# One core: attention by packed keys, then a gated two-layer product, with another table of the order of the same 2739 pieces

## The chip, the cores and the metric

The kernel runs on one core of a Trainium2 chip. The metric is device time in microseconds (us) of one execution. The engines named here are TensorE (PE; its weight loads are shown apart as PEld), VectorE (DVE), ScalarE (ACT) and SyncE (SP), whose only work is to issue the DMAs.

## What is computed

Eight batches of eight heads attend through 32 packed queries `p`: first `p` looks at `k` and `v`, and then `q` looks at what that gave. The rows of all heads side by side are `x` (4608 x 512), which goes through a gated pair of matrix products.

```python
def sm_attn(qq, kk, vv):
    s = scale * np.matmul(qq, kk.transpose(0, 1, 3, 2))
    s = s - np.max(s, axis=-1, keepdims=True)
    a = np.exp(s)
    a = a / (np.sum(a, axis=-1, keepdims=True) + 1e-09)
    return np.matmul(a, vv)
p_packed = sm_attn(p, k, v)          # 8 x 8 x 32 x 64
out = sm_attn(q, p_packed, p_packed) # 8 x 8 x 576 x 64
...
h = x @ w_in                         # 4608 x 2048
sp = np.where(h > 20.0, h, np.log1p(np.exp(np.minimum(h, 20.0))))
g = h * np.tanh(sp)
return (g @ w_out).astype(np.float32)
```

Inputs and output are float32; `w_in` and `w_out` come to the kernel as the 64-bit patterns of doubles and are turned into float32 by it.

## The kernel before

**Pieces and their order.** The function `program()` (L1073) builds a list of 2739 pieces with a `Lineup` (L184). `add` gives each piece its engine, what it reads, writes and takes of buffers, and its number. 904 pieces are for PE, 728 for DVE, 701 for ACT and 406 for SP. `Lineup.sequence` (L216) walks the table `SEQUENCE` (L40 to L176) and issues the pieces in its order. Every engine then carries out its own pieces in that order and nothing else decides: a piece whose input is late holds up all that stands behind it on its engine, and a DMA on SP holds up all DMAs behind it. The tile framework puts the waits in, and hands out the buffer of a kind that became free first.

```python
        for n in numbers:
            if n < 0:
                yield from [fill] * -n
                continue
```

**Fills.** A negative number in the table is that many fills (L1556, L1557): products of the identity with itself into a bank of PSUM that nobody reads. They occupy PE where it would wait. Each shows as two matmul records of 128 columns.

**The attention of a batch.** For batch 0 `first(b)` and for the others `later(b)` add these pieces: `s` (scores, L359), `mx` and `top` on DVE (L402 to L409, the maxima), `tl` on ACT (L312, one tiny exponential that makes ACT fetch its table for exp), `e` on ACT (L421, four exponentials from PSUM), `w` on PE (L452, turning), `a1T` (L478, L481), `pv` (L487, L502), `pp` (L520), `ppTp`/`ppT` (L529, L535), `m` (L540, the matches with `q`), then `rm`, `rl`, `rs2`, `ri`, `wg` on DVE and `e2` on ACT (the second softmax; for batch 1 L617 to L647 with L634 on ACT, for the others L561 to L584 with L571), `tw` (L604) and `aT` (L661, L664).

**The weights.** `fetch` (L698) brings a piece of `w_in` or `w_out`. `up`, `sg`, `rn`, `bd` and `w`/`wi` turn it into float32: `up` L704 and `rn` L714 on ACT, `sg` L708, `bd` L717 and `w` L723 on DVE. `wo` (L742) and L745 split `w_out` into a high and a low part, which are kept in DRAM (`w_f32`, `quarters`, L750 and L755). `again` (L811) brings a piece of `w_in` once more. `pw` (L825) multiplies a piece of `w_in` into the packed values; `wph` (L844, ACT) and `wp` (L849, DVE) split the result into high and low.

**The first two batches** go by blocks. An `up` piece (L884) makes the gate's input; `act` (L890, and L892 for the rest) is the Mish function on ACT; L896 and L900 split it; `down` (L932 to L934) multiplies by `w_out`. `up` writes to one of two PSUM banks in turn, `ps_h` and `ps_x`; `ps_x` also holds the scores of a batch (`s`) until its `e` pieces have read them.

**Batches 2 to 7** go by steps with mixed quarters of `w_out`. `L774` to `L791` make the mixtures from `mix_w` (fetched at L768) with ACT's part at L782 and DVE's at L786, and store them. L798 brings a mixture for each step (`mix`, 512 KB). A step is `sup` (L974), `sx` (L980, ACT) and `sh` (L982), sums (L995 to L999), a split (L1003 on ACT, L1007 on DVE), `sdown` (L938 to L940) and endings (L1027 on ACT, L1033 on DVE), then a send (L1039, L1044).

**Table loads of ACT.** Exp and Mish lie in different tables. A table is loaded ahead of the first activation of the other kind; `tl` pieces stand there so that this load is not made by the `e` or `e2` piece itself.

Of the kernel before, what the change touches and what calls it, by code (L numbers as in the profile page):

```python
# [40 lines left out]
    1, 0, 2, 6, 5, 107, 64, 7, 8, 3, 9, -3, 12, 10, 11, 13, 4, 14, -1, 19, 15, 65, 16, 20, -4, 21, 17, 18, 25, 22, 23,  # L41
    26, 24, 66, 109, 27, 28, 29, 113, 110, -2, 30, 120, 31, 108, -2, 32, 126, 111, 33, 69, 35, 112, 34, 162, 38, 36, 37,
    39, 75, -1, 44, 41, 40, 42, 70, 47, 45, 43, 46, 176, -7, 71, 48, 51, 49, 182, 115, 114, 72, 116, 50, 195, 121, 122,
    -6, 55, 73, 123, 189, 127, 74, 76, 128, 78, 52, 79, 67, 124, 77, 53, 80, 125, 129, -11, 83, 54, 163, 68, 117, 58, 56,
    164, 85, 61, 81, 86, 130, 84, 82, 165, 131, -3, 87, 213, 118, 177, 59, 166, 178, 88, 167, 179, -3, 133, 57, 62, 132,
    183, 63, 60, 136, 184, 134, 119, 137, 185, 135, 168, 233, 191, 138, 190, 186, 170, 192, 193, 253, 196, 194, 140, 139,
    340, 197, 180, 273, 181, 89, 141, 187, 144, 198, 430, 199, 90, 146, 200, 142, 423, 145, 215, 202, 214, 143, 147, 169,
    150, 216, 217, 203, 152, 218, 205, 204, 221, 172, 151, 148, 188, 206, 173, 153, 287, 235, 154, 91, 149, 234, 155,
    219, 237, 156, 236, 92, 254, 174, 238, 157, 158, 299, 220, 239, 255, 207, 159, 93, 201, 209, 208, 257, 256, 240, 223,
    241, 210, 94, 224, 96, 225, 258, 243, 274, 95, 261, 244, 160, 259, 320, 245, 277, 97, 161, 175, 275, 260, 227, 276,  # L50
    98, 211, 229, 228, 288, 99, 278, 263, 291, 100, 281, 226, 279, 417, 230, 246, 369, 280, 300, 264, 231, 212, 265, 289,
    301, 101, 302, 247, 303, 102, 249, 322, 304, 323, 283, 292, 307, 321, 284, 262, 232, 248, 305, 324, 285, 250, 325,
    251, 267, 306, 341, 266, 103, 326, 308, 269, 268, 252, 436, 344, 309, 328, 270, 342, 600, 271, 290, 310, 343, 104,
    370, 418, 419, 345, 105, 286, 327, 420, 311, 272, 346, 329, 330, 348, 424, 425, 347, 171, 331, 426, 484, 106, 350,
    431, 504, 427, 373, 293, 428, 371, 352, 432, 294, 421, 433, 295, 434, 351, 353, 498, 313, 437, 374, 222, 296, 332,
    422, 297, 438, 354, 314, 440, 439, 372, 315, 355, 298, 511, 312, 486, 485, 333, 441, 487, 435, 356, 316, 517, 318,
    488, 443, 429, 357, 604, 499, 500, 365, 319, 501, 366, 505, 506, 529, 334, 489, 507, 508, 492, 336, 513, 335, 539,
    502, 514, 599, 381, 503, 337, 358, 338, 512, 339, 367, 518, 549, 519, 360, 515, 490, 442, 516, 520, 382, 521, 446,
    368, 642, 509, 444, 383, 447, 359, 361, 531, 375, 363, 491, 530, 377, 364, 532, 533, 392, 376, 534, 559, 384, 541,
    540, 537, 385, 445, 601, 542, 543, 393, 522, 378, 379, 394, 544, 550, 380, 387, 547, 386, 535, 551, 402, 643, 552,  # L60
    403, 545, 569, 396, 388, 523, 390, 536, 404, 644, 553, 560, 554, 398, 561, 524, 645, 562, 391, 646, 413, 647, 563,
    397, 414, 648, 555, 564, 395, 399, 650, 649, 406, 400, 557, 570, 605, 408, 401, 407, 546, 746, 454, 527, 556, 525,
    405, 567, 409, 526, 448, 411, 573, 565, 450, 579, 528, 449, 571, 455, 451, 651, 464, 606, 652, 415, 572, 607, 602,
    456, 608, 655, 465, 610, 609, 611, 412, 466, 656, 474, 613, 653, 657, 614, 458, 658, 612, 654, 416, 615, 603, 459,
    460, 452, 453, 457, 317, 574, 747, 461, 510, 581, 580, 462, 468, 582, 463, 470, 469, 478, 471, 659, 480, 475, 750,
    467, 660, 589, 389, 748, 476, 661, 479, 751, 477, 663, 662, 481, 749, 494, 664, 618, 482, 666, 495, 577, 621, 619,
    665, 583, 712, 620, 566, 802, 575, 622, 472, 349, 473, 616, 617, 496, 591, 623, 576, 497, 592, 624, 722, 625, 667,
    626, 584, 713, 671, 627, 723, 590, 672, 674, 706, 668, 628, 673, 708, 884, 707, 483, 714, 629, 709, 818, 724, 410,
    715, 669, 710, 716, 670, 711, 718, 717, 630, 732, 719, 726, 675, 742, 727, 728, 720, 679, 721, 631, 733, 593, 680,
    682, 725, 594, 803, 632, 597, 734, 681, 729, 633, 883, 758, 548, 242, 736, 676, 738, 585, 677, 743, 730, 806, 678,  # L70
# [101 lines left out]
    2686, 2622, 2680, 2694, 2688, 2623, 2689, 2624, 2695, 2690, 2681, 2696, 2625, 2703, 2682, 2626, 2691, 2665, 2704,  # L172
    2666, 2692, 2698, 2705, 2699, 2706, 2700, 2708, 2713, 2709, 2710, 2714, 2701, 2717, 2702, 2711, 2718, 2712, 2715,
    2721, 2722, 2719, 2723, 2725, 2726, 2729, 2727, 2731, 2730, 2716, 2733, 2720, 2735, 2724, 2732, 2728, 2737, 2734,
    2736, 2738,
)  # L176

F64_SCALE = 2.0 ** -112
# [1453 lines left out]
```

## Time and profile before

| what | value |
|---|---|
| time of the runs | 693.58, 691.81, 692.48 us; median 692.48 |
| span of the profiled execution | 691.1 us |
| time of its own for the profiled execution | none shown; its span is 1.4 us under the median of the runs |
| PE busy | 674.8 us, 98% |
| DVE busy | 501.7 us, 73% |
| ACT busy | 409.3 us, 59% |
| moved by DMA | 200.26 MB, mean 290 GB/s |

The span is from the first to the last instruction that the profiler saw. Busy times of different engines overlap each other. Matmuls on PE are pipelined: the next one starts before the one before it has ended, so the start-to-start time is what one costs.

### The profile page before, as it was taken

The page shows a single profiled execution, that of the slowest core. Times are in us where ns is not written, and L with a number is a line of the kernel's source. Part 1 is how long each engine was busy: PE and PEld are TensorE (multiplying, and loading weights), DVE is VectorE, ACT ScalarE, POOL GpSimd, SP SyncE. Part 2 cuts the span into 40 slices and gives each one's busy share as a digit, 9 for nine tenths or more (in the row PEclk, how much of TensorE's full clock was granted, in tenths as well). Part 3 has the DMA queues.
Part 4 walks back from the last instruction along what each step waited for, and adds up shares of the span by engine and source line. Part 5 has one row for each costly group of instructions (what it writes and reads, how often), then busy time and mean ns, then how long its engine had stood idle before and what let it go on. Part 6 is the DMA issues. An engine that isn't in the chain of part 4 may idle for free.

```text
span 691.1 us, 15614 instructions
## 1 busy us (share of the span) xinstructions
PE 674.8 (98%) x6144; PEld 611.1 (88%) x6144; DVE 501.7 (73%) x999; ACT 409.3 (59%) x900; POOL 0.7 (0%) x6
## 2 busy tenths in 40 slices
PE   8889999999999999999999999999999999999997
PEld 5668787778789999999999999899999999899996
DVE  2999996788655786578886686868766777665674
ACT  4899998554543655556666465666555545444552
POOL 0000000000000000000000000000000000000000
PEclk9999999999999999999999999999999999999999
DMA  8998999999999977794989827787496918481866
GB/s 300 402 407 294 345 378 355 328 347 344 370 397 418 386 238 305 251 359 155 346 280 340 307 103 265 296 287 292 141 403 221 360 44 294 151 289 60 312 204 216
DMA packets 70569, 200.26 MB, mean 290 GB/s; under 512 B 7776, under 2 KB 22112, under 8 KB 70496
## 3 DMA queue, kind: packets, MB, share of 16 engines
q1 hardware_dynamic: 70496, 199.26, 79.2%
q8 instruction: 49, 0.80, 0.4%
q14 instruction: 24, 0.20, 0.1%
HBM read 164.63 MB, written 34.60 MB: 288 GB/s over the span
## 4 chain that ended last, share of the span: by engine, by line
PE 78%; DMA 12%; DVE 4%; ACT 3%; issue 1%; SPq 0%; DVEq 0%; ACTq 0%
PE ps_h L974 20%; PE acc L938 13%; PE acc L939 12%; PE acc L940 12%; PE ps_h L884 5%; DMA mix<-mixed 4%; PE ps_w L825 4%; PE acc L932 3%; PE acc L933 3%; PE acc L934 3%; DMA mixed<-mix_o 2%; DMA w_out_f<-wo 1%; PE ps_s L359 1%; DMA xT<-in_q_rest_dram 1%; DMA wi<-w_in_f 1%; DMA xT<-in_q_main_dram 1%
## 5 line engine op out<-in xcount | busy, mean ns | idle before, releaser
L938 PE MATMUL acc<-mix,mixed_split 128*128 128x256 f32 x784 | 225.1, 287 | 1.3 <-DMA mix<-mixed 1.0
L939 PE MATMUL acc<-mix,mixed_split 128*128 128x256 f32 x784 | 221.7, 283 | 0.0
L940 PE MATMUL acc<-mix,mixed_split 128*128 128x256 f32 x784 | 221.6, 283 | 0.0
L974 PE MATMUL ps_h<-aT_hi,wp 128*128 128x256 f32 (+1 forms) x768 | 174.0, 297 | 0.0
L1007 DVE TENSOR_TENSOR mixed_split<-x,mixed_split 128x896 fp32r<-128x896 f32 x112 | 121.6, 1088 | 58.9 <-ACT mixed_split L1003 57.9
L938 PEld LDWEIGHTS acc<-mix,mixed_split 128*128 128x128 f32 x784 | 149.8, 191 | 15.0 <-issue 10.0
L1003 ACT CAST mixed_split<-x 128x896 fp32r<-128x896 f32 x112 | 105.3, 941 | 85.2 <-DVE x L999 47.6
L940 PEld LDWEIGHTS acc<-mix,mixed_split 128*128 128x128 f32 x784 | 150.2, 192 | 0.0
L939 PEld LDWEIGHTS acc<-mix,mixed_split 128*128 128x128 f32 x784 | 150.0, 191 | 0.0
L980 ACT ACTIVATE x<-ps_h 128x256 f32<-128x256 f32 x192 | 72.5, 384 | 101.9 <-PE ps_h L974 97.8
L974 PEld LDWEIGHTS ps_h<-aT_hi,wp 128*128 128x128 f32 x768 | 131.2, 190 | 0.6 <-issue 0.5
L974 PE MATMUL ps_h<-aT_lo,wp 128*128 128x320 f32 (+1 forms) x384 | 113.6, 296 | 0.0
L995 DVE TENSOR_TENSOR x<-x 128x128 f32<-128x128 f32 x112 | 32.0, 286 | 59.2 <-ACT x L980 58.0
L974 PEld LDWEIGHTS ps_h<-aT_lo,wp 128*128 128x128 f32 x384 | 73.0, 190 | 0.1
L884 PE MATMUL ps_h<-aT_hi,wp 128*128 128x288 f32 x256 | 58.8, 299 | 4.6 <-ACT g L890 1.6
L884 PEld LDWEIGHTS ps_h<-aT_hi,wp 128*128 128x128 f32 x256 | 43.5, 188 | 11.0 <-ACT wp L844 2.1
L932 PE MATMUL acc<-wo,split 128*128 128x512 f32 x128 | 51.4, 402 | 0.0
L996 DVE TENSOR_TENSOR x<-x 128x256 f32<-128x256 f32 x112 | 47.6, 425 | 5.0
L933 PE MATMUL acc<-wo,split 128*128 128x512 f32 x128 | 50.2, 392 | 0.0
L934 PE MATMUL acc<-wo,split 128*128 128x512 f32 x128 | 50.1, 392 | 0.0
L849 DVE TENSOR_TENSOR wp<-ps_w,wp 128x512 fp32r<-128x512 f32 x64 | 42.2, 681 | 8.9 <-ACT wp L844 8.7
L1033 DVE TENSOR_TENSOR o<-acc,o 128x256 f32<-128x256 f32 x98 | 38.7, 416 | 10.5 <-PE acc L940 8.3
(106 smaller groups left out, 822.9 us busy)
## 6 DMA issues: line engine op xcount, KB each, us to landing
mix<-mixed SPq DMA_DIRECT2D x141, 512.0 KB, 6.8
wi<-w_in_f SPq DMA_DIRECT2D x56, 512.0 KB, 7.5
mix<-shared SPq DMA_DIRECT2D x17, 512.0 KB, 8.9
xT<-in_k_main_dram SPq DMA_DIRECT2D x16, 512.0 KB, 5.8
v<-in_v_main_dram SPq DMA_DIRECT2D x16, 512.0 KB, 8.1
w_st<-in_w_in_dram SPq DMA_DIRECT2D x16, 512.0 KB, 7.4
xT<-in_q_main_dram SPq DMA_DIRECT2D x16, 512.0 KB, 7.9
w_st<-in_w_out_dram SPq DMA_DIRECT2D x16, 512.0 KB, 7.9
```

The costliest lines, as they stand in the source:

```text
L884: nc.tensor.matmul(out=ps, lhsT=w[:, fs], rhs=a[:, g, cs], start=(n == 0), stop=(n == 5))
L932: nc.tensor.matmul(out=acc, lhsT=hi[:, cs], rhs=wh, start=start, stop=False)
L933: nc.tensor.matmul(out=acc, lhsT=hi[:, cs], rhs=wl, start=False, stop=False)
L934: nc.tensor.matmul(out=acc, lhsT=lo[:, cs], rhs=wh, start=False, stop=stop)
L938: nc.tensor.matmul(out=acc, lhsT=hi, rhs=w[:, 0], start=start, stop=False)
L939: nc.tensor.matmul(out=acc, lhsT=hi, rhs=w[:, 1], start=False, stop=False)
L940: nc.tensor.matmul(out=acc, lhsT=lo, rhs=w[:, 0], start=False, stop=stop)
L974: nc.tensor.matmul(out=ps, lhsT=w[:, fs], rhs=x[:, g, a:e], start=(n == 0), stop=(n == 5))
L980: nc.scalar.activation(out=self.x[:, at:at + 2].rearrange("p c t -> p (c t)"), in_=self.ps[i][:, :m], func=AF.Mish)
L996: nc.vector.tensor_tensor(out=x[:, 1:3], in0=x[:, 3:8:4], in1=x[:, 6:7].to_broadcast([P, 2, P]), op=ALU.subtract)
L1003: nc.scalar.copy(out=self.split[:, 0], in_=self.x[:, :7])
L1007: nc.vector.tensor_tensor(out=x[:, 1], in0=self.x[:, :7], in1=x[:, 0].bitcast(F32), op=ALU.subtract)
```

## The change

Only the table `SEQUENCE` is another one. It holds the same 2739 pieces, each once; the code, the buffers and the dependencies are as they were. The fills are 27 in 9 places in place of 43 in 11. Of the pieces, 501 of 904 on PE keep their order among each other, 459 of 701 on ACT, 412 of 728 on DVE and 237 of 406 on SP. On PE no piece moves by more than 11 places.

```diff
@@ -38,141 +38,147 @@
 SEQUENCE = (
-    1, 0, 2, 6, 5, 107, 64, 7, 8, 3, 9, -3, 12, 10, 11, 13, 4, 14, -1, 19, 15, 65, 16, 20, -4, 21, 17, 18, 25, 22, 23,
-    26, 24, 66, 109, 27, 28, 29, 113, 110, -2, 30, 120, 31, 108, -2, 32, 126, 111, 33, 69, 35, 112, 34, 162, 38, 36, 37,
-    39, 75, -1, 44, 41, 40, 42, 70, 47, 45, 43, 46, 176, -7, 71, 48, 51, 49, 182, 115, 114, 72, 116, 50, 195, 121, 122,
-    -6, 55, 73, 123, 189, 127, 74, 76, 128, 78, 52, 79, 67, 124, 77, 53, 80, 125, 129, -11, 83, 54, 163, 68, 117, 58, 56,
-    164, 85, 61, 81, 86, 130, 84, 82, 165, 131, -3, 87, 213, 118, 177, 59, 166, 178, 88, 167, 179, -3, 133, 57, 62, 132,
-    183, 63, 60, 136, 184, 134, 119, 137, 185, 135, 168, 233, 191, 138, 190, 186, 170, 192, 193, 253, 196, 194, 140, 139,
-    340, 197, 180, 273, 181, 89, 141, 187, 144, 198, 430, 199, 90, 146, 200, 142, 423, 145, 215, 202, 214, 143, 147, 169,
...
-    460, 452, 453, 457, 317, 574, 747, 461, 510, 581, 580, 462, 468, 582, 463, 470, 469, 478, 471, 659, 480, 475, 750,
-    467, 660, 589, 389, 748, 476, 661, 479, 751, 477, 663, 662, 481, 749, 494, 664, 618, 482, 666, 495, 577, 621, 619,
-    665, 583, 712, 620, 566, 802, 575, 622, 472, 349, 473, 616, 617, 496, 591, 623, 576, 497, 592, 624, 722, 625, 667,
...
-    1251, 1230, 1249, 1252, 1255, 1250, 1167, 1257, 1256, 1253, 1163, 1168, 1272, 1258, 1259, 1169, 1265, 1203, 1166,
...
-    1504, 1597, 1500, 1443, 1508, 1505, 1521, 1531, 1605, 1444, 1506, 1512, 1513, 1509, 1608, 1514, 1510, 1445, 1517,
-    1446, 1609, 1515, 1447, 1518, 1448, 1610, 1516, 1527, 1519, 1611, 1522, 1523, 1520, 1606, 1449, 1524, 1528, 1450,
...
+    1, 0, 2, -1, 7, 5, 8, 9, 10, 11, -1, 12, 13, 14, 6, 15, 16, 19, -3, 21, 23, 17, 20, 18, 25, 22, 107, 24, 109,
+    26, 27, 28, 3, 29, -1, 30, 108, 31, 111, 110, -1, 32, 112, 33, 4, 35, 113, 115, 64, 34, 36, 37, 38, 44, 39, 41,
+    40, 42, 45, 114, 75, 117, 47, 48, 65, 43, 66, 46, 96, 116, 118, 120, 51, 126, 122, 121, -6, 71, 72, 73, 123,
+    127, 128, 74, 129, 76, 80, 78, 162, 124, 69, 77, 79, 49, 164, 165, 176, 50, -11, 55, 56, 52, 83, 81, 70, 53,
+    125, 54, -2, 58, 163, 61, 85, 84, 178, 179, 86, 82, 182, 189, 59, 130, 177, 87, 88, 417, 166, 195, 131, 183,
+    167, 184, 185, 57, -1, 133, 62, 60, 191, 180, 213, 136, 137, 134, 63, 135, 138, 192, 140, 190, 139, 67, 68, 181,
+    196, 193, 273, 89, 197, 198, 186, 144, 141, 90, 187, 146, 199, 194, 200, 215, 142, 143, 202, 168, 169, 145, 214,
...
+    453, 467, 460, 494, 459, 468, 461, 746, 574, 579, 602, 575, 470, 581, 576, 462, 582, 463, 580, 469, 747, 471,
+    472, 478, 480, 750, 658, 659, 479, 476, 657, 481, 751, 748, 663, 749, 583, 473, 654, 603, 495, 496, 523, 664,
+    616, 712, 618, 620, 660, 477, 706, 621, 619, 713, 565, 714, 584, 617, 538, 622, 661, 585, 666, 578, 665, 587,
...
+    1167, 1272, 1168, 1169, 1170, 410, 1249, 1254, 1172, 1173, 1273, 1283, 1284, 1175, 1259, 1261, 1203, 1174, 1176,
+    1265, 1260, 1266, 1267, 1268, 1250, 1262, 1294, 1274, 1276, 1204, 1275, 1269, 1277, 1179, 1182, 1270, 1181,
...
+    1449, 1617, 1618, 1450, 1632, 1548, 1633, 1549, 1550, 1551, 1553, 1636, 1637, 1547, 1624, 2122, 1552, 1638,
...
```

Some stretches of the two tables, read engine by engine (number:piece; the batch, block or step stands first in the brackets):

```
SP, first DMAs
before  1:k(0,0) 0:pT(0) 2:k(0,1) 6:v(0,1) 5:v(0,0) 107:fetch(0) 64:pT(1) 3:q(0,0) 4:q(0,1) 65:k(1,0) 66:k(1,1) 113:fetch(1) 120:fetch(2) 126:fetch(3)
after   1:k(0,0) 0:pT(0) 2:k(0,1) 5:v(0,0) 6:v(0,1) 107:fetch(0) 3:q(0,0) 4:q(0,1) 113:fetch(1) 64:pT(1) 65:k(1,0) 66:k(1,1) 120:fetch(2) 126:fetch(3)
ACT, from the second softmax of batch 0 to the first gates
before  47:e2(0) 51:e2(0) 114:up(1) 116:rn(1) 121:up(2) 123:rn(2) 127:up(3) 78,79,77,80:e(1) 129:rn(3) 163:up(4) 56:aT 85,84:a1T(1) 165:rn(4) 177:up(5) 59:aT 88:pp(1) 179:rn(5) 62:aT 183:up(6) 136,134:wph(0) 185:rn(6) 168:wo(0) 190:up(7) 192:rn(7) 196:up(8) 139:act(0) 141:act(0) 198:rn(8) 90:ppT(1) 142:gh(0)
after   114:up(1) 75:tl(1,0) 47:e2(0) 96:tl(1,1) 116:rn(1) 51:e2(0) 121:up(2) 123:rn(2) 127:up(3) 129:rn(3) 80,78,77,79:e(1) 165:rn(4) 56:aT 163:up(4) 85,84:a1T(1) 179:rn(5) 59:aT 177:up(5) 88:pp(1) 183:up(6) 185:rn(6) 62:aT 136,134:wph(0) 192:rn(7) 190:up(7) 139:act(0) 196:up(8) 198:rn(8) 141:act(0) 90:ppT(1) 142:gh(0) 168:wo(0)
DVE, second softmax of batch 0
before  39:rm 40:rl 42:rm 45:rm 43:rl 46:rl 48:rs2 49:ri 115:sg(1) 72:mx(1)
after   115:sg(1) 39:rm 40:rl 42:rm 45:rm 117:bd(1) 48:rs2 43:rl 46:rl 118:w(1) 122:sg(2) 72:mx(1)
PE, around w(2)
before  747:pw(6) 468:up(18,0) 470:up(18,1) 478:up(19,0) 480:up(19,1) 475:down(15,1) 467:down(14,3) 476:down(15,2) 477:down(15,3) 494:down(16,0) 618:w(2)
after   747:pw(6) 478:up(19,0) 480:up(19,1) 476:down(15,2) 495:down(16,1) 496:down(16,2) 712:down(17,0) 618:w(2)
PE, scores of batch 4 to the next piece that takes ps_x
before  1167:s(4) 1253:sdown(15,2) 1272:sdown(16,0) 1265:sup(19,0) 1283:sdown(17,0) 1273:sdown(16,1) 1254:sdown(15,3) 1274:sdown(16,2) 1294:sdown(18,0) 1267:sup(19,1)
after   1167:s(4) 1272:sdown(16,0) 1254:sdown(15,3) 1273:sdown(16,1) 1283:sdown(17,0) 1284:sdown(17,1) 1265:sup(19,0) 1267:sup(19,1)
ACT, exponentials of batch 4
before  1266:sx(19) 1171:tl(4,0) 1173,1174,1176,1175:e(4) 1268:sx(19)
after   1238:sh(17) 1249:sh(18) 1173,1175,1174,1176:e(4) 1266:sx(19) 1268:sx(19)
PE, from the piece that frees the buffer of mixture 1450 to the piece that uses it
before  1520:sdown(34,3) [14 pieces, 9.0 us of PE] 1632:sdown(39,0)
after   1520:sdown(34,3) [20 pieces, 14.5 us of PE] 1632:sdown(39,0)
SP, around the piece of w_in fetched again for pw(10)
before  790:send quarters(7) 829:again(10) 787:send quarters(4) quarters(5) 830:again(11) 781:send 927:mix(0,1) 928:mix(0,2)
after   927:mix(0,1) 928:mix(0,2) quarters(7) rk(0) quarters(7) 929:mix(0,3) 930,931:mix(1) 781:send 932:mix(1,2) 829:again(10) 830:again(11) 933:mix(2,0)
```

The `tl` pieces stand elsewhere too: in the table after, `e` of batches 3, 4, 6 and 7 and `e2` of batches 3 to 7 have no `tl` directly ahead of them that would load their table, and three `tl` pieces stand between Mish pieces. By the order of the pieces on ACT, its table has to be changed 33 times where it was 27 (with one load at the start that both have, 28 loads are in the profile of before).

## Rows read from the trace of the kernel before

**Rows 1.** The page: busy time, share and instructions of each engine.

```profile
PE 674.8 (98%) x6144; PEld 611.1 (88%) x6144; DVE 501.7 (73%) x999; ACT 409.3 (59%) x900; POOL 0.7 (0%) x6
```

**Rows 2.** Busy time by stretch: start:end, length, engines, granted PE clock, DMA share, GB/s.

```profile
34.60:51.80 17.20, 14.77 (x125) 11.80 (x126) 16.41 (x33) 16.50 (x37) 0.00 (x0) 1.00 1.03 406
...
34.00:36.00 2.00, 0.67 (x3) 0.44 (x4) 1.68 (x4) 2.00 (x4) 0.00 (x0) 1.00 1.01 351
```

**Rows 3.** Waits of PE up to 42 us: waited for, us in total, times, longest.

```profile
PE ps_h L884 <- ACT g L890: 1.6, 1, 1.6
...
PE ps_h L884 <- ACT wp L844: 1.2, 1, 1.2
PE ps_h L884 <- DVE wp L849: 0.8, 1, 0.8
```

**Rows 4.** Waits of PE after 42 us, all of them.

```profile
PE acc L938 <- DMA mix<-mixed: 1.0, 3, 0.5
PE ps_a L452 <- DVE wp L849: 0.8, 1, 0.8
PE ps_h L884 <- ACT g_rest L892: 0.5, 2, 0.3
PE ps_h L884 <- ACT a L421: 0.5, 1, 0.5
PE acc L938 <- DVE o L1033: 0.2, 1, 0.2
```

**Rows 5.** ACT in order of time, 19 to 39 us: start, length, instruction, idle before.

```profile
19.58 0.63 ACT L634 ACTIVATE a<-a 128x512 f32<-128x512 f32 x1 [1.58 <-DVE a L623]
...
35.02 0.62 ACT L742 CAST wo<-wo 128x512 fp32r<-128x512 f32 x1
35.51 0.70 ACT L704 ACTIVATE wi<-w_st 128x512 f32<-128x512 f32 x1
...
36.90 0.65 ACT L704 ACTIVATE wi<-w_st 128x512 f32<-128x512 f32 x1
37.57 1.28 ACT L890 ACT_TABLE_LOAD   x1
38.86 0.66 ACT L890 ACTIVATE g<-ps_h 128x288 f32<-128x288 f32 x2
```

**Rows 6.** PE in order of time, at 39, 41, 126, 193, 278 and 286 us.

```profile
39.33 0.40 PE L884 MATMUL ps_h<-aT_hi,wp 128*128 128x288 f32 x1 [1.65 <-ACT g L890]
...
41.12 1.09 PE L825 MATMUL ps_w<-wi,ppT 64*32 64x512 f32 x16
...
126.43 1.09 PE L452 MATMUL ps_a<-ident,a 128*128 128x128 f32 x8 [0.82 <-DVE wp L849]
...
193.88 1.95 PE L825 MATMUL ps_w<-wi,ppT 64*32 64x512 f32 x32
...
278.77 1.31 PE L359 MATMUL ps_s<-xT,pT 64*32 64x256 f32 x32
...
286.59 0.28 PE L974 MATMUL ps_h<-aT_hi,wp 128*128 128x256 f32 x1
```

**Rows 7.** DVE in order of time, at 122 us.

```profile
122.97 0.69 DVE L774 TENSOR_TENSOR mix_t<-mix_w 128x512 f32<-128x512 f32 x1 [3.35 <-DMA mix_w<-w_out_f]
```

**Rows 8.** The chain that ended last: start, length, what (a mixture at 361 us).

```profile
360.94 9.09 DMA mix<-mixed
```

**Rows 9.** DVE and ACT in order of time around the exponentials of batch 4.

```profile
282.65 0.17 DVE L409 TENSOR_SCALAR top<-top 128x2 f32<-128x2 f32 x1
...
285.67 0.53 ACT L421 ACTIVATE a<-ps_s,top 128x320 f32<-128x320 f32 x1
```

**Rows 10.** SP in order of time, at 183 us.

```profile
183.01 1.59 SPq L811 DMA_DIRECT2D wi<-w_in_f x2
```

**Rows 11.** The page: DMA issues: out<-in, engine, op, count, KB each, median us to landing.

```profile
wi<-w_in_f SPq DMA_DIRECT2D x56, 512.0 KB, 7.5
```

**Rows 12.** DVE in order of time, from 681 us.

```profile
684.39 2.66 DVE L1033 TENSOR_TENSOR o<-acc,o 128x256 f32<-128x256 f32 x7 [4.36 <-PE acc L940]
```

250 rows, old and new, of the table SEQUENCE are left out of this document.

## The prediction

> **What bounds the kernel now.** I read the busy times first: PE is busy for 674.8 us of the 691.1 us span [rows 1], so a new order can only win what PE loses to waits, and can lose whatever it adds to them. Second, the stretches: from 34.6 to 51.8 us PE is busy for 14.77 of 17.20 us while ACT and DVE are nearly full (16.50 and 16.41) [rows 2]. There the chain through ACT sets the pace. Third, the waits of PE, parted at 42 us. Before it, three waits between 33 and 40 us are on ACT's and DVE's work on the first packed weights and gates: 1.6, 1.2 and 0.8 us [rows 3]. After it there are eight waits of together 3.0 us [rows 4]. That view counts from the modelled end of the matmul before; by starts, each costs some 0.16 us more (the wait of 0.82 us at 126.43 us is one of 0.98), so the eight cost about 4.3 us. This is nearly all that the order after 42 us has to give: the rest of PE's time is products that both tables hold, and switches between kinds of products, as many of them in either.
>
> **What the change does, part by part.**
>
> *The start.* After the second softmax of batch 0 the order before puts, between the split of the first packed weights and the first gate, two `rn`, one `wo`, two `up` and the table load on ACT. The new table takes `wo(0)` out and puts `up(8)` behind the first gate. By starts, `wo` costs 35.51 - 35.02 = 0.49 us (the next piece follows at once) and `up` 37.57 - 36.90 = 0.67 us [rows 5]; the pieces of `rn` only change places. Further ahead, `up(1)` and `rn(1)` move into holes in which ACT waits for the softmax's first step on DVE (1.58 us before 19.58) [rows 5]. They would give 1.2 us, but `sg(1)`, `bd(1)` and `w(1)` now stand among the softmax pieces on DVE and take most of that back; walking both engines piece by piece with durations of their rows, I keep 0.35 us. So the first gate comes at 38.86 - 0.49 - 0.67 - 0.35 = 37.35 us. The second gate of that pair is now behind `up(8)` and `rn(8)`, at 37.35 + 0.33 + 1.31 = 38.99, and frees `ps_x` some 0.47 us later, at 39.46. Before, PE went through that block without a second stop, from 39.33 to `pw(1)` at 41.12, so its second half, 0.89 us, began at 40.23 [rows 6]. The difference is **-0.77 us**. Nothing hides this, as PE waits here; how long it lasts is decided by whether `fetch(1)` lands in time, since `sg(1)` reads it at the head of DVE's softmax. `fetch(1)` moves ahead of three transfers on SP, so it should. The bounds: both holes used and no delay of the softmax, a gain of 0.77 + 0.85 = 1.6 us; or `sg(1)` held for some 0.8 us, a gain of nought.
>
> *Sixteen fills less.* They stand in waits. Where the wait is longer than they are they cost nothing, and their going gains nothing: 0, with bounds of 0 and -0.5 us.
>
> *Mixtures that came late.* Three waits of 1.0 us together are for a mixture of 512 KB [rows 4]. At 361 us a transfer takes 9.09 us from issue to landing, [rows 8], with 9.0 us of PE pieces between the release of its buffer and its use: it lands just too late. The new table has 14.5 us of pieces there, and similarly 17.3 for 10.8 us at the second such wait (595 us). Two of three go; the third, the last mixture of all, has 9.0 us of PE work in both tables. **-0.96 us** (of the 1.0 + 3 x 0.16 us, the part of the first two, 0.42 and 0.54).
>
> *Waits behind mix_w.* At 122.97 us DVE had stood for 3.35 us at a difference, waiting for `mix_w` [rows 7], with the low half of `wp` behind it, for which PE's turning `w(2)` stood 0.82 us [rows 6]. An earlier such wait held the maxima of batch 2, hence the exponentials and `ps_x`, 0.5 us [rows 4]. In the new table those differences stand later against their fetches by 0.5 to 6 us of work, with one exception (three us, after the last of those waits). I take both as gone, -0.98 and -0.56 (0.5 with its 0.16, shorter by rounding), and of the two waits on `g_rest` half, -0.2: **-1.74 us**. But `w(2)` stands only 4.3 us of PE work behind `pw(6)`, where it was 6.6; the bound on the other side is that it keeps its whole wait.
>
> *Table loads.* ACT changes its table 33 instead of 27 times, at 1.28 us each [rows 5]: 7.7 us more on an engine with 40% to spare [rows 1]. Three pairs stand in stretches where ACT has idle time, and are costed at nothing; the cover is the idle time of ACT between gates. The other side is what has lost its `tl`. The next piece on `ps_x` after the scores of batch 4 comes 3.96 us of PE work after them, and was at 286.59 with scores until 278.77 + 1.31 = 280.08, so 6.5 us [rows 6]. The chain that must fit is maxima and top (in the trace until 282.82, with DVE's endings between them; about 1.5 us alone), four exponentials (at most 0.53 us each, overlapping a little, 1.9 us) [rows 9], and now the load, if it begins only after `top`: 3.4 + 1.28 = 4.6 us. It overruns by 0.7 us in batch 4, and is even in batches 6 and 7 (4.68 us of cover). Where the load goes ahead of the wait, it costs nothing. I take **+0.7 us**; bounds 0 and +3.
>
> The Trainium skill, page "ScalarE: Activation LUTs", section "What ACT_TABLE_LOAD costs", gives 1283 ns for the load plus about 1380 ns of drain, 2.66 us a switch. The trace's load agrees, but the activation after it starts 1.29 us after the load's start (38.86 - 37.57) [rows 5], so no such drain follows it here; by the page's total the overrun of batch 4 would be 2.1 us rather than 0.7 and the sum 1.4 us worse.
>
> *w_in fetched again for pw(10).* The two transfers left SP from 183.01 for 1.59 us [rows 10]; a transfer of `wi` takes a median of 7.5 us from issue to landing [rows 11], so the second landed before 192, and `pw(10)` began at 193.88 [rows 6], some 2 us to spare. The new table puts five to eight mixtures ahead. At 406 GB/s [rows 2] a mixture is 1.3 us, 6 to 10 us in all, against a queue whose mixtures may leave as soon as their buffers are free, so much of it moves into time that SP spent waiting. Bounds 0 and +6, taken **+0.2** (the row nearest: it had landed before `pw` was reached).
>
> *The end.* The last endings run 684.39 to 687.05 [rows 12] and the same pieces stand there, but one that was between them is now earlier, so the chain hangs on an earlier piece: **+0.2 us**, bounds 0 and +0.4.
>
> Sum: -0.77 - 0.96 - 1.74 + 0.7 + 0.2 + 0.2 = -2.37 us on the span, 691.1 to 688.7 us. The profiled execution stands 1.4 us under the median of the runs, 692.48, so the median comes to 692.48 - 2.37 = **690.1 us**, -0.34%. About 0.3%, 2.1 us, is what a measurement of this kernel can tell from no change.
>
> **The rivals.**
>
> *Given back.* The eight waits are what is left of many places where margins are near nought, and a table of other margins makes new ones of the same size: 4.3 us before, 4.3 us after, less the start and the added terms. For it: PE's distance from scores to the next `ps_x` piece falls in batches 4 to 7, and from `pw(6)` to `w(2)`. Against it: most mixtures get longer distances. It gives -0.77 + 0.2 = -0.6, 691.9 us.
>
> *Slower by table loads.* One mechanism: an `e` or `e2` piece without `tl` starts the load after DVE's result, with DVE's endings (0.41 us each) in between as in batch 4. Then scores to exponentials takes 4.6 + 0.8 = 5.4 us against a cover of 4 to 4.7, and the second softmax carries 1.28 us likewise. Four `e` and five `e2` pieces at 0.7 to 1.3 us are up to 9 x 1.0 = 9 us. It decides once more than 5 of those nine reach PE: the forecast without its +0.7 is -3.1, and 6 x 1.0 turns it into +2.9, 695.4 us. For it: ACT's place in the scores' chain is fixed. Against it: PE has `sdown` pieces to do in batches 3 to 7 and its own waits there were for transfers alone [rows 4].
>
> *The clock.* With 16 fills fewer, PE is idle longer before 33 us. The trace shows a granted clock of 1.00 (2.4 GHz) even from 34 to 36 us, with 0.67 of 2.00 us busy [rows 2], so I see no sign that it falls. If it fell to 1.2 GHz from 24 to 34 us, the scores, turnings and values there (some 4 us at full clock) would take 4 us more, half of it hidden by ACT: +2, 692.1 us. The Trainium skill, page "TensorE: Matmul & The Clock Gate", section "Part 1: The HAM clock gate", has an idle PE fall back to half its clock; by it the fewer fills could do this, and rows 2 show no such fall at the idlest stretch.
>
> **How the numbers follow.** Forecast 0.48 (its own range 688.3 to 691.3), given back 0.33, slower by table loads or by the late `pw(10)` 0.13, the clock 0.06. Half of the forecast's neighbourhood lies on either side of the bound of 0.3% (690.4), but the early gain and the mixtures may be larger than taken (to -5 us if every wait goes: 687.2), which is why faster gets 0.48, and same the given back, the clock and the slower half: 0.40; slower 0.12. The range runs from 687.2 to 694.2, leaving out part of the slower case and the extreme of the gain.
>
> **What would show it.** First gate near 37.4 us and `pw(1)` near 40.3; no wait for `wp` at `w(2)`, one DMA wait left in the waits of PE after 42 us; 33 or 34 table loads, and a wait on `a` L421 of less than 1 us in batch 4. A first gate after 38.9 would make the start wrong (`fetch(1)` late), more than 2 us of waits on ACT after 180 us the table term, a wait for `wi` at `pw(10)` the queue term, and a clock below 1.00 before 40 us the fills.

## The result, and the profile after

The changed kernel takes **697.2 us** (median of 4 runs, 696.5 to 699.08) against 692.64 us before (4 runs): 1.0066 times, interval 1.0046 to 1.0085. The forecast of 690.1 us (687.2 to 694.2) had the wrong sign; of its rivals the one with table loads, 695.4 us, came nearest.

The page of the kernel after (columns as in [rows 1]). All lines of its code stand six lower than before.

```profile
span 696.0 us, 15527 instructions
...
PE 677.0 (97%) x6112; PEld 610.8 (88%) x6112; DVE 502.1 (72%) x999; ACT 419.9 (60%) x906; POOL 0.7 (0%) x6
```

PE's work is nearly the same; the span is 4.9 us longer. Much of where it went the waits of PE after 42 us say, beside [rows 4]:

```profile
PE ps_h L980 <- ACT a L427: 1.8, 3, 0.8
PE ps_h L890 <- ACT g L896: 1.5, 2, 1.0
PE ps_h L890 <- DVE wp L855: 1.0, 1, 1.0
PE acc L944 <- DMA mix<-mixed: 0.9, 1, 0.9
PE ps_h L890 <- ACT a L427: 0.5, 2, 0.3
```

Of [rows 4], the wait at `w(2)`, those on `g_rest`, the one on an ending and two of the three on mixtures are gone. The forecast had these, of `g_rest` the half, but no term for the ending. In their place PE waits for exponentials (`a` L427) in five places, for gates and for `wp`. One of the five, 0.2 us at 118.79, is that of batch 2, which the forecast took as gone (0.5 us in [rows 4]); 2.3 us behind it PE waits 0.6 us more, for a gate. The groups of ACT show who loads the tables now (before: 13 by `tl`, none by L421 or L571):

```profile
L986 ACT ACT_TABLE_LOAD x11 | 14.1, 1283 | 1.4 <-PE ps_h L980 1.2
L896 ACT ACT_TABLE_LOAD x6 | 7.7, 1283 | 0.1
L577 ACT ACT_TABLE_LOAD x6 | 7.7, 1283 | 0.1
L318 ACT ACT_TABLE_LOAD x6 | 7.7, 1283 | 0.1
L427 ACT ACT_TABLE_LOAD x4 | 5.1, 1283 | 8.5 <-DVE top L415 8.5
```

Ten loads are made by an `e` or `e2` piece itself (one of them for batch 1). The four of L427, in batches 3, 4, 6 and 7, begin only after the wait for `top` is over, which the 8.5 us of idle time say. Batch 4, ACT and then PE in order of time, beside [rows 9]:

```profile
285.42 1.28 ACT L427 ACT_TABLE_LOAD   x1 [1.76 <-DVE top L415]
286.71 0.47 ACT L427 ACTIVATE a<-ps_s,top 128x256 f32<-128x256 f32 x1
...
287.68 0.47 ACT L427 ACTIVATE a<-ps_s,top 128x256 f32<-128x256 f32 x1
...
288.13 0.53 ACT L427 ACTIVATE a<-ps_s,top 128x320 f32<-128x320 f32 x1
```

```profile
288.29 0.39 PE L980 MATMUL ps_h<-aT_hi,wp 128*128 128x256 f32 x1 [0.76 <-ACT a L427]
```

ACT stands idle for 1.76 us until `top` is there, and only then spends 1.28 us on the table, and PE has waited. By the code the two exponentials of 256 columns read `ps_x`, those of 320 another bank. In batches 4 and 6 the table of before has both of 256 first and the changed one has them first and third, so `ps_x` comes free after the third, at 288.15, and not after the second. By the length of one exponential that may be up to 0.5 us of the wait in each of these batches. No run put this order alone back, so its share is not shown.

In this profile the start went the other way than forecast too. Busy time by stretch of the kernel after (columns as in [rows 2]; the granted clock is the third number from the end):

```profile
20.00:22.00 2.00, 1.62 (x32) 0.49 (x18) 2.00 (x6) 0.89 (x4) 0.00 (x0) 0.85 1.02 391
22.00:24.00 2.00, 2.00 (x11) 1.37 (x7) 2.00 (x4) 2.00 (x4) 0.00 (x0) 0.50 1.05 424
...
36.00:38.00 2.00, 2.00 (x8) 1.78 (x9) 2.00 (x5) 1.98 (x3) 0.00 (x0) 0.50 1.06 370
38.00:40.00 2.00, 2.00 (x11) 1.99 (x10) 1.50 (x4) 1.99 (x6) 0.00 (x0) 0.50 1.00 393
```

TensorE runs at 1.2 GHz where the granted clock is 0.50, and the first gates' products take twice as long there. ACT in order of time shows a second thing, a wait of the second high copy of `pw(0)` for a low difference of the other half:

```profile
33.57 0.62 ACT L850 CAST wp<-ps_w 128x512 fp32r<-128x512 f32 x1
35.14 0.59 ACT L850 CAST wp<-ps_w 128x512 fp32r<-128x512 f32 x1 [0.94 <-DVE wp L855]
...
38.24 0.41 ACT L896 ACTIVATE g<-ps_h 128x288 f32<-128x288 f32 x1
```

The first gate came at 38.24 (38.86 in [rows 5], 37.35 forecast).

**A common measure.** Each matmul of a trace was matched to its piece, so that the times at which PE has done the same amount of work can be compared. This is how far each profiled execution moved against the profile of before (us, + is later), by stretches bounded by the times of that profile:

```
                     0-48   48-172  172-198  198-365  365-end   sum
changed kernel      +1.14   -2.08   +3.21    +1.35    +0.89   +4.51
before again        +2.07   -1.11   +0.49    +0.02    -0.84   +0.63
tl back             +2.47   -1.69   +2.15    +0.14    -0.32   +2.75
tl, pairs back      +1.28   -1.14   +2.67    +0.15    -0.44   +2.52
... + softmax of 2  +1.29   -0.93   +2.03    +0.15    -0.82   +1.72
before without tl   +1.38   -1.78   +1.20    +0.14    +2.38   +3.32
before, then changed +0.30  -1.81   +0.01    +0.13    -1.58   -2.95
```

The second row is the same kernel twice: its own start differs by 2 us from one execution to the next, and half of this is taken back up to 172 us; 1.0 us of that is the wait at `w(2)`, which this execution does not have. So the two first columns say little about an order. The three later ones say more, but here too one execution differs from another of the same kernel by 0.5 us from 172 to 198 us and by 0.8 us behind 365 us.

### The profile page after: what moved, and what is told of

It reads as the page before. It is cut to its first block, busy times and chain, and to the rows that moved or that the text cites. A ratio compares the mean times of both kernels' runs of the same rounds, so it can differ in the third digit from the quotient of the medians.

```text
span 696.0 us, 15527 instructions
## 1 busy us (share of the span) xinstructions
PE 677.0 (97%) x6112; PEld 610.8 (88%) x6112; DVE 502.1 (72%) x999; ACT 419.9 (60%) x906; POOL 0.7 (0%) x6
## 4 chain that ended last, share of the span: by engine, by line
PE 66%; DVE 3%; ACT 2%; DMA 1%; issue 0%; DVEq 0%; ACTq 0%
PE ps_h L980 22%; PE acc L944 13%; PE acc L945 12%; PE acc L946 12%; PE ps_w L831 3%; DMA mix<-mixed 1%; ACT a L427 1%; PE ps_m L365 1%; DVE mx L408 1%; PE ps_pp L493 1%; ACT L427 1%; PE ps_a L458 1%; DVE mixed_split L1013 0%; DVE wp L855 0%; DVE o L1039 0%; PE acc L938 0%
## 5 line engine op out<-in xcount | busy, mean ns | idle before, releaser
L980 PE MATMUL ps_h<-aT_hi,wp 128*128 128x256 f32 (+1 forms) x768 | 175.3, 298 | 1.8 <-ACT a L427 1.8
L980 PEld LDWEIGHTS ps_h<-aT_hi,wp 128*128 128x128 f32 x768 | 131.3, 189 | 5.1 <-ACT a L427 2.4
L980 PE MATMUL ps_h<-aT_lo,wp 128*128 128x320 f32 (+1 forms) x384 | 113.6, 296 | 0.0
L980 PEld LDWEIGHTS ps_h<-aT_lo,wp 128*128 128x128 f32 x384 | 72.9, 190 | 0.1
L1001 DVE TENSOR_TENSOR x<-x 128x128 f32<-128x128 f32 x112 | 32.2, 287 | 52.2 <-ACT x L986 50.8
L890 PE MATMUL ps_h<-aT_hi,wp 128*128 128x288 f32 x256 | 61.5, 310 | 5.3 <-ACT wp L850 2.3
L890 PEld LDWEIGHTS ps_h<-aT_hi,wp 128*128 128x128 f32 x256 | 45.3, 196 | 14.6 <-ACT wp L850 3.2
```

Of the source, the lines that this page charges most:

```text
L890: nc.tensor.matmul(out=ps, lhsT=w[:, fs], rhs=a[:, g, cs], start=(n == 0), stop=(n == 5))
L980: nc.tensor.matmul(out=ps, lhsT=w[:, fs], rhs=x[:, g, a:e], start=(n == 0), stop=(n == 5))
```

## The experiments

Each edit is one of the table; of the pieces that a diff doesn't name, the order is that of the kernel named. The code is the same in all.

**Loads of the table.** The first run puts the `tl` pieces back:

```diff
 (changed table; batches 2 to 7)
-1238:sh(17) 1249:sh(18) 1173:e(4) 1175:e(4)
+1238:sh(17) 1249:sh(18) 1171:tl(4,0) 1173:e(4) 1175:e(4)
```

> The changed table with one thing put back: each tl piece of batches 2 to 7 stands directly ahead of the e or e2 piece of its batch, so ACT's table is changed 27 times again and no e or e2 piece of batches 2 to 7 makes its own load. Theory (the loads behind top hold ps_x): the waits of PE on the exponentials in batches 3, 4, 6 and 7 (0.47, 0.92, 0.70 and 0.70 us by starts in the trace of the changed kernel) go, 2.8 us in all: about 694.4 us by the runs of the changed kernel, 1.0025 of before, and the span near 693.2. Rival (they only stand where PE would have waited for something else): the next piece waits in their place and less than 0.8 us is gained.

Measured: 694.64 us, 1.0038 (1.002 to 1.0056) of before. The waits of PE after 42 us:

```profile
PE ps_h L884 <- ACT g L890: 1.8, 2, 1.3
PE acc L938 <- DMA mix<-mixed: 1.4, 1, 1.4
PE ps_h L884 <- ACT a L421: 0.7, 1, 0.7
PE ps_h L884 <- DVE wp L849: 0.2, 1, 0.2
```

The three waits of `ps_h L980 <- ACT a` are gone, and so is the one of batch 3. Batches 4, 6 and 7 win 0.9 us each in the comparison by work, which counts PE's restart too, and nothing takes their place before the last mixture, which is 0.5 us later. The theory held. The other kept traces bear it out: PE's waits at the next piece on `ps_x` in batches 3, 4, 6 and 7 (0.47, 0.92, 0.70 and 0.70 us by starts) stand within 0.03 us in all five profiles with the changed `tl` pieces (four of them from runs further down), and those of batches 4, 6 and 7 in none of the eight in which `tl` is put back.

Whether a missing `tl` costs by itself was asked of the kernel before:

```diff
 (before; batches 3 to 7)
+610:tl(2,0) 894:tl(3,0) 915:tl(3,1) ... 2143:tl(7,1)
-1266:sx(19) 1171:tl(4,0) 1173:e(4)
+1266:sx(19) 1173:e(4)
```

> The kernel before with the ten tl pieces of batches 3 to 7 taken to where batch 2's first stands, so that each e and e2 of batches 3 to 7 makes its own load of the table; the number of loads stays 28. Theory (a load behind top costs only where the next piece on ps_x stands near the scores): before has 5.0 us and more of PE work there, against 4.6 to 5.4 us for maxima, load and exponentials, so PE waits less than 1 us in all, and the time is 692 to 693 us, 1.000 to 1.0015 of before. Rival (the loads alone cost what was lost in batches 3, 4, 6 and 7): about 2.8 us more, 1.004.

697.94 us, 1.007 (1.0041 to 1.0099). It does not answer its question: the eleven `tl` in a row took ACT 2.55 us ahead of batch 2's exponentials, and PE waited 3.0 us there. Batches 3, 6 and 7 still lost about 1 us each. A run that leaves batch 2 as it was:

```diff
 (before; b = 3 to 7)
-tl(b,0) ahead of e(b), tl(b,1) ahead of e2(b)
+both directly behind e2(b-1)
```

> The kernel before with the two tl pieces of each of batches 3 to 7 moved to right behind the e2 of the batch before, where ACT still has the table of exp, so that no load is made ahead of an e or e2 of these batches; 28 loads as before, none of them early. (The run that put all ten in one place held ACT for 2.6 us at batch 2 and could not be read there.) Theory, after that run: batches 3, 6 and 7 lose about 1 us each at the next piece on ps_x or behind it, batch 4 and 5 nothing, 3 us in all, 1.004. Rival (before's distances hide the load): under 0.7 us, 1.001 or less.

696.14 us, 1.0047 (1.0031 to 1.0063). Waits of PE after 42 us, and ACT at batch 6:

```profile
PE acc L938 <- DMA mix<-mixed: 1.4, 2, 0.9
PE ps_h L974 <- ACT x L980: 1.2, 2, 0.7
PE ps_h L974 <- ACT g L890: 0.9, 1, 0.9
PE ps_h L884 <- ACT a L421: 0.6, 1, 0.6
PE acc L938 <- DVE o L1033: 0.3, 1, 0.3
```

```profile
456.59 1.28 ACT L980 ACT_TABLE_LOAD   x1
457.88 0.66 ACT L980 ACTIVATE x<-ps_h 128x256 f32<-128x256 f32 x2
```

So it costs about 3 us in the order of before alone, in batches 3, 6 and 7, and not at the exponentials' own bank: the load of the other table starts 1.29 us later than before by work, and the next gates behind it (`g` L890 in batch 3, `x` L980 in 6 and 7) come too late for PE. The rival is out. The distance of `ps_x` matters all the same: in the order of before PE has 4.2 to 5.4 us of work between the scores and the next piece on that bank and does not wait there, in the changed one 3.4 to 4.7 us, and there it does. But distance alone does not make a missing `tl` free.

**Pairs of copies.**

```diff
 (changed table; 17 packed pieces)
-136:wph(0) 137:wp(0) 134:wph(0) 135:wp(0)
+136:wph(0) 134:wph(0) 137:wp(0) 135:wp(0)
```

> The changed table with one thing put back: in 17 of the 32 packed pieces of w_in the two high copies on ACT (wph) stand ahead of the two low differences on DVE (wp) again, where the changed table has high, low, high, low. Theory (with a low difference between them, the second high copy has a wait on DVE that it needs not have): ACT's waits of 0.94 us at 35.14, 0.76 at 44.83 and 1.01 at 185.88 go, the first up piece starts about 1 us earlier and the wait of 1.1 us of up(31,0) goes: 1.1 to 2 us less, some 695.5 us. Rival (the second copy waits for its buffer or for the product, whatever the order): the same waits stand under another name, no change.

697.51 us, 1.0074 (1.0055 to 1.0093), no gain that the runs show. ACT's waits on `wp` are gone as the theory said, the first up starts at 34.63 instead of 35.77, but the next product waits 0.99 us for the low difference, and ACT's waits for mixtures' stores ahead of its high copies grow from 1.9 us to 4.1 us in all. Both repairs together:

> The changed table with both repairs, tl ahead of its e and e2 and high copies together, and nothing else. Theory: batches 4, 6 and 7 without their 0.9 us each (2.8 in all), and of what was lost between 165 and 200 us about 1 us less; the waits of up(29,0) and up(31,0), 1 us each, stay, since the buffers of wp come free late there: 693.5 to 694.5 us, about 1.002 to 1.003. Rival (pairs did all in 165 to 200 us): 1.000 or less.

694.18 us, 1.0034 (1.0016 to 1.0052). The waits at `up(29,0)` and `up(31,0)` stay, 1 us each.

**The start and the clock.** The fills of before in the changed table, its own fills and 13 more, and before's whole start:

```diff
 (changed table; x3: 43 fills where before has them)
-... -6 71:s(1) -11 55:tw(0)
+... -7 71:s(1) -6 55:tw(0) -11 83:w(1)
 (changed table; x8: 13 fills more)
-71:s(1)          138:up(0,0)
+-5 71:s(1)    -8 138:up(0,0)
```

> The changed table with the 43 fills of before, each run of them ahead of the same piece of PE as there, in place of its 27. Theory (the granted clock fell in 20 to 25 and 35 to 42 us because PE had too little to do ahead of it): the clock stays at 1.00 up to 42 us, the first blocks run at full clock and pw(1) comes at about 41.4 in place of 42.26; about 0.8 us less. Rival (the fall comes from the two long waits, for k ahead of the scores of batch 1 and for wp ahead of the first up, of which the second has no fills in either table): the clock still falls at 35 us, and less than 0.4 us is gained. A second rival: the 16 fills hold up real pieces and the time goes up.

699.5 us, 1.0103 (1.0075 to 1.0131): the time went up, as the second rival says. The clock fell at 27.9 us, just ahead of a run of 11 fills, which took 4.04 us instead of the 2.62 us that as many took in the profile of before, with real pieces behind them. What else made this start late was not followed.

> The changed table with 13 more fills: 5 ahead of the scores of batch 1, where PE waited 1.3 us, and 8 ahead of the first up, where it waited 2.3 us. Theory (the clock falls where PE stood idle ahead): the clock stays at 1.00 from 20 to 42 us, pw(1) comes at 41.4 instead of 42.3, about 0.9 us less: 696.3. Rival (the clock falls although PE has fills, as it did in the run with 43 fills): it falls to 0.50 in at least one stretch, and nothing is gained.

696.35 us, 1.0045 (1.0026 to 1.0065), and the clock fell to 0.50 from 28.8 to 32.2 us; but it was up when the first gates' products ran. The time is that of the theory and the fall that of the rival, so the run does not part them.

> The table of before up to pw(1), with its fills, and behind it all other pieces in the order of the changed table. Theory (the stretches add up): what the changed table lost up to pw(1), 1.14 us, is won back and stays won: span near 694.9, about 696.1 us in the runs. Rival (transfers set the pace up to 200 us, and a late start is absorbed there): less than 0.3 us of change at 200 us and at the end.

698.98 us, 1.0104 (1.0084 to 1.0124). The table of before up to 41 us, and the clock still fell at 37 us, so the question of the stretches is not answered. A second profile of the kernel before:

> The kernel before once more, for a second profile of it. The run with the early part of before had the same pieces in the same order up to pw(1) and still showed the granted clock at 0.50 from 37.0 to 43.8 us, which the one profile of before does not. Theory (whether the clock falls in the first 45 us differs from one execution to the next, also in the kernel before): this profile may show a fall to 0.50 between 20 and 45 us, with pw(1) 1 to 2 us later than 41.1 and the span longer by that, and the runs spread over some 3 us. Rival (only the changed order makes it fall): the clock is 1.00 up to the end, pw(1) at 41.1 as before. The time is that of before, ratio 1.000 within 0.002.

693.18 us, 1.001 (0.9988 to 1.0031). Its stretches:

```profile
30.00:34.00 4.00, 3.33 (x102) 2.05 (x102) 3.67 (x9) 4.00 (x11) 0.00 (x0) 1.00 1.04 412
34.00:38.00 4.00, 2.57 (x14) 2.21 (x14) 3.40 (x8) 3.94 (x8) 0.00 (x0) 0.88 1.02 376
38.00:42.00 4.00, 2.85 (x13) 2.57 (x12) 3.83 (x9) 3.87 (x9) 0.00 (x0) 0.50 1.03 415
```

The same kernel, and here the clock falls to 1.2 GHz after PE stood idle, which the first profile doesn't show. This execution is 2 us later at 48 us and 0.6 us at the end. So the fall is not the change's alone, and 43 fills do not prevent it. The runs say how much it can be worth, as each lists its mean granted clock: of 129 executions of the kernel before (689.5 to 696.7 us), 16 show 1.000 with a median of 691.4 us, and 58 show 0.995 or less with a median of 693.8 us. The four of the changed kernel show 0.991 to 0.995, at 697.2 us; at a like clock it is still more than 3 us slower.

**The rest of 172 to 198 us, and seams.** Three versions join pieces of both tables:

```diff
 (x7: before up to pw(1), then the changed order; tl and pairs back)
 (x9: changed up to up(24,1), then before; tl back)
 (x10: as x9, from sup(3,1) on changed again; tl and pairs back)
```

> The table of before up to pw(1) with its fills, the order of the changed table behind it, with tl directly ahead of its e and e2 in batches 2 to 7, and both high copies ahead of the low differences in the 17 packed pieces. Theory (behind 47 us the changed table lost 3.4 us by the two causes alone and wins by its longer distances): behind 47 us it loses 3.4 - 3.1 (tl) - 2.1 (pairs) = -1.8 us, a span of 689 to 690 if the clock stays, 0.9975 of before; 2 us more if the clock falls as with the early part of before alone. Rival (the two repairs win back the same waits, or the shift makes others): no better than 1.000.

695.86 us, 1.0044 (1.0025 to 1.0063), the rival's side: the clock fell at the start, and 172 to 198 us lost 2.8 us, nearly as in the changed kernel.

> The changed table up to up(24,1), at about 153 us, and behind it all other pieces in the order of before, with tl ahead of each e and e2 of batches 2 to 7. Theory (the changed table wins up to 150 us and loses behind it): from 48 to 153 us it wins 1 to 2 us on before, as the changed kernel did (its lead went from -1.14 to +0.2, counted with the start), and nothing is lost behind; 0.5 to 1.5 us under before when the clock falls alike in both, 0.998 to 1.000. Rival (what it wins up to 150 us is only its late start being absorbed by the waits for transfers, as in the second profile of before, which fell from +2.08 to +0.8 there): nothing is won, 1.000 to 1.002.

> As that, but only the stretch from up(24,1) to sup(3,1), some 153 to 205 us, in the order of before; the changed order ahead of it and behind it, with tl ahead of its e and e2 and both high copies ahead of the low differences in the 17 packed pieces. Theory (three causes: loads, pairs, and the stretch around pw(8), pw(9) and the scores of batch 3, where the mixture fetched late holds the buffers of wp): all losses behind 47 us are gone and the mixtures' gain of about 1 us stays: 1 to 3 us under before, 0.996 to 0.999. Rival (the losses are what is left of margins in any order): about before's time, 1.000.

700.75 us, 1.0116 (1.0091 to 1.014), and 698.51 us, 1.0095 (1.0068 to 1.0121). The first is for x9, the second for x10. Neither answers its question: at the seam the second softmax of batch 2, which the changed table has 20 us later, is done in one go, and PE waits 4.5 us for a gate behind it. Behind the seam x10 loses nothing and wins 1.4 us. It pointed at that softmax:

```diff
 (tl and pairs back; DVE)
-699:mt(7) 633:rs2(2) 634:ri(2) 704:ml(7) 635:wg(2) 701:ml(7)
+699:mt(7) 704:ml(7) 701:ml(7)
```

> The changed table with tl and pairs put back, and in addition the second softmax of batch 2 (rm, rl, tl, e2, rs2, ri, wg) where before has it, some 20 us earlier than the changed table. Theory (those DVE and ACT pieces, in 174 to 178 us of the changed kernel, hold up the last mixture, whose store holds the buffers that the high copies of pw(8) and pw(9) wait for): the waits of PE at up(29,0) and up(31,0), 1 us each, fall to under 0.4 us each, 1.2 to 2 us less than with tl and pairs alone, near 692.5 us, 1.000 to 1.001 of before. Rival (the mixture is late because its fetch waited 4.1 us on SP for a buffer, whatever DVE does): the two waits stay.

694.03 us, 1.0012 (0.9997 to 1.0026). Half of it at most: the wait at `up(29,0)` goes from 0.98 to 0.54 us by starts, that of `up(31,0)` stays at 1.14, and the interval overlaps that of both repairs alone. Two tries at that one:

```diff
 (x15: as x12; PE)
-844:up(30,1) 852:up(31,0) 890:s(3) 860:down(28,1)
+844:up(30,1) 890:s(3) 860:down(28,1) 852:up(31,0)
 (x16: as x12; ACT)
-825:wph(9) 827:wph(9) 640:aT(2) 843:act(30) 845:act(30)
+825:wph(9) 843:act(30) 827:wph(9) 845:act(30) 640:aT(2)
```

> As the run with the second softmax of batch 2 put back, with one piece more put back: up(31,0) stands behind the scores of batch 3 and down(28,1), as in the kernel before, where the changed table has it directly behind up(30,1). Theory (up(31,0) takes the bank that act(30) frees, and act(30) stands on ACT behind the high copies of pw(9), which wait for the buffers of the last mixture's stores; before has seven pieces of PE between up(30,1) and up(31,0), the changed table none): the wait of 1.14 us of up(31,0) goes, 0.8 to 1.1 us less than that run, span 692.1 to 692.4 with the same clock, 1.000 of before. Rival (PE waits for act(30) or its followers at the next piece anyway): the wait moves to up(31,1) or to the first step, less than 0.3 us gained.

> As the run with the second softmax of batch 2 put back (up(31,0) again where the changed table has it), but on ACT the first half of act(30) stands ahead of the second high copy of pw(9), and its second half ahead of the split of the turned matches. Theory (up(31,0) waits because act(30) is queued on ACT behind a high copy that waits for a mixture's store): the first half of act(30) comes at 185.8 in place of 187.65 us of that run's trace, the wait of 1.14 us of up(31,0) goes, and the scores behind it wait less than 0.5: about 0.8 us less, near 692.4 in the span with the same clock. Rival (the wait moves on, as in the last run, where it went to the scores): less than 0.3 us.

For x15 696.2 us, 1.0054 (1.0024 to 1.0083): the wait went on to the scores, 1.5 us, and the clock fell behind it (0.51 from 189 to 192.5 us). And for x16 694.71 us, 1.0039 (1.0022 to 1.0057), with as much lost in this stretch as before the edit (2.09 us against 2.03, by work): `up(31,0)` no longer waits, the scores wait 0.6 us for `wp` instead. The rivals held both times. By the traces the high copies of `pw(8)` and `pw(9)` stand for buffers that mixtures' stores release; which step makes those stores late, and whether that is all of this stretch, is not settled.

**The part of the forecast that held.**

```diff
 (x14: before up to m(3), 228 us, then the changed order; tl and pairs back)
```

> The table of before up to m(3), some 228 us, and the changed order behind it, with tl ahead of its e and e2 and the high copies together. Theory (behind 230 us the changed order is the better one once tl is back): the waits for mixtures at 370 and 595 us and for the ending at 565 us go, 1.3 us, and the last mixture takes 0 to 1 us back: 0.3 to 1.3 us under before, 0.998 to 0.9995. Rival (the last mixture's wait grows by all that was won): 1.000.

691.1 us against 692.65, 0.9985 (0.9968 to 1.0003), with a span of 688.5 us. Its waits of PE after 42 us, all of them:

```profile
PE ps_h L884 <- ACT a L421: 0.5, 1, 0.5
PE acc L938 <- DMA mix<-mixed: 0.2, 1, 0.2
```

Behind 230 us it wins 1.5 us on the first profile of before: the waits for mixtures at 370 and 595 us and for the ending at 565 us are gone, without losing anything at the loads. On the second profile of before it wins 0.6 us there, as that one has no wait at 595 us and next to none for the last mixture. It has the lowest time of all versions, though the interval still touches no change.

## Why the prediction was wrong

*Table loads* is the step that failed. It took +0.7 us with bounds of 0 and +3. The changed kernel lost 2.8 us to them by starts: 0.47, 0.92, 0.70 and 0.70 us in batches 3, 4, 6 and 7, where the sum had 0.7 for batch 4, "even" for 6 and 7, and nothing for 3. The path was the right one, a load behind `top` that holds `ps_x`; the chain and the cover were mis-sized. The chain was put at 4.6 us from the end of the scores (its terms, 3.4 and 1.28, give 4.7). Until PE could go on it measured 4.9 us in batch 4 and 5.4 us in 6 and 7, since other pieces stand in it: two endings of DVE in batch 6, one of ACT in batch 7. And batch 3 was left out without a reason, though its cover is the shortest, 3.4 us; by the prediction's own chain it would have added over a us. The cover of batch 4 before was misread too: the next piece on `ps_x` is not the row at 286.59 but this one, so it was 5.4 us and not 6.5:

```profile
285.51 0.28 PE L974 MATMUL ps_h<-aT_hi,wp 128*128 128x256 f32 x1
```

The prediction also counted the chain only to the end of the exponentials. The run of before without `tl` shows a second path, on which the load back delays the gates and PE waits even where `ps_x` has cover.

The rival of the table loads had the mechanism right, but its sum came near partly by luck. It wanted more than five of nine loads to reach PE at about 1 us each; four did, all of `e` pieces, and the five of `e2` pieces cost PE nothing that the waits show. Other terms made up the rest.

*The stretch from 172 to 198 us* had no term but +0.2 for `pw(10)`, and lost 3.2 us. `pw(10)` itself did not wait in any profile, so the taken +0.2 was not needed. Of what was lost there, `tl back` takes away about 1 us, 0.47 us of it the wait for the exponentials of batch 3; some 0.6 us goes, by single executions, with the second softmax of batch 2 (moved by 20 us beside the last mixture); and a rest is open. The prediction had seen the one difference of a mixture that now stands three us less behind its fetch and set it aside as behind the last wait; DVE stood 2.8 us for it, and buffers of `wp` wait on that mixture's stores.

*The start.* Forecast -0.77. The profile shows +1.14 against the first of before and -0.9 against the second, and the clock falls in the kernel before too. Over all kept profiles nothing of the forecast's size is left: `pw(1)` begins at 41.1 to 45.1 us, median 42.3, in the seven with the start of before, and at 41.0 to 43.6 us, median 42.3, in the nine with the changed start and its own fills (six of them with the high copies together). One step is wrong for certain: the two copies of `pw(0)`, between which a low difference now stands, were taken as before, and the second waited 0.94 us. The clock as a rival got a chance of 0.06 and was tied to the fills; the profiles show falls with 27, 40 and 43 of them.

*Mixtures, mix_w and g_rest.* Forecast -2.7 us, and these waits are gone from the trace of the changed kernel. But much of it was the price of a single execution. The wait at 370 us (0.42 us) stands in all five profiles that have the order of before there, and in none with the changed order: that part held. The 0.54 us at 595 us and the 0.98 us at `w(2)` stand only in the first of five profiles of that order (a wait at `w(2)` also once behind the changed order), so their going is no gain that the change can be credited with. The wait for the exponentials of batch 2 was not gone, as said above.

*The end* was +0.2, and it measures +0.36: from PE's last product on, 4.66 us in all five profiles with the end of before and 5.02 in that of the changed kernel. The wait for the last mixture, which the prediction left as it was, is another matter: 0.5 us in the first profile of before and 0.9 in that of the changed kernel by the views, and it varied by 1 us among the executions with the order of before.

An estimate of the whole from these rows: 2.8 to 3.4 us of loads (without and with PE's restart), about 2 us for the rest of 172 to 198 us, 0.4 at the end, less 0.8 for the wait at 370 us and the ending at 565 us, is 4.4 to 5.0 us; the runs have 4.6.

The rival *given back*, 691.9 us, has the right picture of small margins, without the size.

## What to carry to other kernels

When an order by hand is replaced, first list what each engine does besides its pieces: table loads, waits that come from the order of issue. A piece that exists only to prefetch something is not interchangeable with its like in another place. And before a part of a microsecond is argued about, take a second profile of the kernel before; here it differed from the first by 2 us at 48 us, and two of the waits that the forecast counted on winning were not in it.

## What was not expected of the hardware

A table load made by the activation itself can be late as well as early. In the four `e` pieces it starts only when the wait for DVE is over (in batch 4 1.76 us idle, then 1.28 us of load), while one ahead of it runs in the idle time. The `e2` piece of batch 6 in the same trace loads at once and waits afterwards:

```profile
482.37 1.28 ACT L577 ACT_TABLE_LOAD   x1
484.09 1.17 ACT L577 ACTIVATE a<-a 128x1152 f32<-128x1152 f32 x1 [0.43 <-DVE a L573]
```

What decides between the two was not tested. The Trainium skill, page "ScalarE: Activation LUTs", section "What ACT_TABLE_LOAD costs", adds 1380 ns of drain to the load; here the activation in batch 4 follows 1.29 us after the load's start (285.42 to 286.71), and the trace shows no such drain.

The granted clock fell to 0.50 for some us before 46 us in the profile of the changed kernel and in all sixteen of the experiments, and in four of those once more between 124 and 193 us; in the first profile of before, alone of the eighteen kept, not before the end. By the runs above such an execution is about one in eight, and the prediction rested on it. The Trainium skill, page "TensorE: Matmul & The Clock Gate", section "Part 1: The HAM clock gate", says that an idle PE falls back to half its clock; the stretches of the second profile of before agree, since the fall follows idle time of PE (0.57 of 2.00 us busy from 34 to 36 us), but the first profile had nearly the same idle time there (0.67 of 2.00 [rows 2]) and no fall.
